# Attention maxima and sums handed over without DRAM, bulk transfers in pieces of 256 KB, and w1's stored parts in longer runs

## The chip, the cores and the metric

The kernel runs on one core of a Trainium2 chip. The core has five engines with a queue of instructions each: TensorE (PE; its weight loads are listed as PEld), VectorE (DVE), ScalarE (ACT), GpSimd (POOL) and SyncE (SP). Every DMA of this kernel is issued by SP. An engine works through its own queue in order, and waits for another engine or for a DMA by a semaphore. The metric is the time on the device of one execution, in microseconds (us), less is better.

## The reference

One transformer layer with an attention branch and an MLP branch that both start from the same normalized input and are added to the input. S = 2048 rows, D = 512 columns, H = 32 heads of 16, F = 1792 hidden units; all inputs and the output are float32.

```python
xn = _layernorm(x, axis=-1)
return x + _A_ref(xn, wqkv, wo) + _B_ref(xn, w1, b1, w2, b2)

# _A_ref
qkv = (xn @ wqkv).reshape(B, S, 3, H, Dh)                # q, k, v by head
scores = einsum("bhqd,bhkd->bhqk", q, k) * (Dh ** -0.5)
p = softmax(scores, axis=-1)
o = einsum("bhqk,bhkd->bhqd", p, v)
return o.reshape(B, S, D) @ wo

# _B_ref
h = gelu(xn @ w1 + b1)                                   # tanh form
return h @ w2 + b2
```

## The kernel before

**Numbers.** Products run in float16, with each float32 operand split into a high and a low part (suffix: index 0 and 1 of the dimension of 2), and three of the four part products are summed (`PAIRS`). The probabilities and v are multiplied in float32.

**Attention by tiles and units.** The 32 heads are taken in 8 groups of 4 (`NG`), the 2048 queries in 4 blocks of 512 (`NQB`): 32 *tiles* t = (g, qb). A tile has 16 *units*, 512 units in all (`NU`). Each unit does two things, for two different tiles. The first (`s_half`, four times) multiplies 128 queries with 512 keys and takes the row maxima with DVE (`mt`, L250). The second (`e_half`, four times) computes the scores again, transposed (128 keys by 512 queries, `pT`), and ACT takes the exponential (L295); `v_half` then multiplies by v into the bank `pV`. The second lags the first by `LEAD` = 20 units, so a tile's 16 units of maxima are done 4 units before its exponentials begin.

**How the maxima get there.** The maximum has to be subtracted from transposed scores, where it differs from column to column. It is done inside the product: the operand `qst` has for each head 64 rows, of which 62 and 63 hold the negative maximum in two float16 parts, and the same rows of `kst` hold the constant `MROW`. At a tile's last unit `s_end` reduces `mt` (128x64) to `mneg` (128x16). One slot later `store` (L264) transposes it on PE with two small products against `ident`, DVE writes the two parts `mhl` (L271, L272), two DMAs store them to DRAM (`m_d`, L275), and when these have landed four DMAs (L280) read rows 62 and 63 of the four heads back. The first `pT` product of the tile waits for them.

**How the sums get there.** v has a 17th column of ones, so row 16 of each head in `pV` is the sum of exponentials. `v_end` copies `pV` to `osb` (ACT, L321). Then, each in a slot of its own: `sums` (four DMAs to `den_d`, L333), a load of all sums as 64x32 into `dn` (L360), `inverse` (DVE, L336, and a store to `den_d`, L338), `spread` (four DMAs that copy each head's 512 reciprocals to 32 partitions of `rb`, L342), `store` (three steps on POOL, L346 to L348, result `ot`) and `put` (L353, to `ot_d`). `n` and `far` (L358) give the distances: 1, 2, 7, 10 and 13 slots after the tile's end, and 1, 2, 3, 5 and 7 in the last group of heads.

**Order.** From the 17th unit on the order on all five engines is written out by hand. `unit` (L582) emits one unit; `tick` (L226) follows each unit: it runs what `later(n, fn)` put down for this slot, then as many POOL steps of the list `pooled` as fit into `POOL_NS` = 2500 ns. A slot is a place in the program and no clock: SP issues an entry as soon as it has got there in its queue and what the entry reads or overwrites is free. `flush` (L231) ends a phase: it runs ticks with no unit between them until no local entry is left.

**What fills the PE beside attention.** `dense` puts up to four products per half unit of a `Group` into the half of the PE array that `v_half` leaves free. Three phases: the projections of q and k with `rest` (L853), beside which `prepare` (L880) loads, scales and splits w1, w2 and wo in 16 chunks of 512 KB (`chunk`, L641; three POOL steps each, L875 to L877) and stores the parts (`put`, L911: w1 to `w1_d`, w2 to `w2_d`); the MLP (`mlp`, L938), with its loads `fetch_x` (L532), `fetch_w1` (L537) and L971; and the product with wo (`tail`, L1072), whose operands `load_o` (L1005) reads for one block of 512 queries at a time in 8 DMAs, when `fetch_o` (L1065) finds that the block's last tile has been stored. `project` (L474) writes q and k by way of the buffers `stg`.

The first 16 units, with layer norm, transposition of x and the first projection, are ordered by the framework's own scheduler.

Of the kernel before, what the change touches and what calls it, by code (L numbers as in the profile page):

```python
# [8 lines left out]
F32 = mybir.dt.float32  # L9
# [38 lines left out]
def layer_kernel(ctx: ExitStack, tc: tile.TileContext, x, wqkv, wo, w1, b1, w2, b2, out):  # L48
# [16 lines left out]
    w1_d = dram.tile([NF, P, 2, NC, P], F16, name="w1_d")  # L65
    w2_d = dram.tile([P, 2, NF, D], F16, name="w2_d")
    acc_d = dram.tile([S, D], F32, name="acc_d")
    m_d = dram.tile([NG * NQB, 16, 2, P], F16, name="m_d")
    ot_d = dram.tile([D, 2, S], F16, name="ot_d")
    den_d = dram.tile([NG * NQB, 2, 4, QB], F32, name="den_d")  # L70
# [26 lines left out]
    mnegs = [const.tile([P, 32], F32, name=f"mneg{i}") for i in range(2)]  # L97
    for m in mnegs:
        nc.gpsimd.memset(m, 0.0)
# [153 lines left out]
    def s_end(u):  # L253
# [7 lines left out]
        nc.vector.tensor_reduce(mneg[:, :16], mt_of[t].rearrange("p h t k -> p (h t) k"), axis=AX.X, op=ALU.max, negate=True)  # L261
        given("dve", 220)

        def store():  # L264

            pt = banks("S")
            for a in range(2):
                nc.tensor.matmul(pt[32 * a:32 * a + 32, :64], mneg[64 * a:64 * a + 64, :],
                                 ident[64 * a:64 * a + 64, 64 * a:64 * a + 64], start=True, stop=True)
            mhl = work.tile([64, 2, 64], F16, name="mhl", bufs=2)  # L270
            nc.vector.tensor_scalar_mul(mhl[:, 0], pt[:64, :64], 1.0 / MROW)  # L271
            nc.vector.scalar_tensor_tensor(mhl[:, 1], pt[:64, :64], 1.0 / MROW, mhl[:, 0], op0=ALU.mult, op1=ALU.subtract)  # L272
            given("dve", 300)
            for a in range(2):
                nc.sync.dma_start(m_d[t, :, :, 64 * a:64 * a + 64], mhl[32 * a:32 * a + 16])  # L275
            for p in range(2):
                for a in range(2):
                    h = 2 * p + a
                    dst = qs[p][qb][64 * a + 62:64 * a + 64, :].rearrange("r (t q) -> r t q", q=P)
                    nc.sync.dma_start(dst, m_d[t, 4 * h:4 * h + 4].rearrange("t r q -> r t q"))  # L280
# [30 lines left out]
    def v_end(u):  # L311
# [19 lines left out]
        def sums():  # L331
            for h in range(4):
                nc.sync.dma_start(den_d[t, 0, h:h + 1, :], osb[32 * h + DH:32 * h + DH + 1, :])  # L333

        def inverse():
            nc.vector.reciprocal(dn, dn)  # L336
            given("dve", 330)
            later(1, lambda: nc.sync.dma_start(den_d[t, 1].rearrange("h (c q) -> (h c) q", q=32), dn))  # L338

        def spread():  # L340
            for h in range(4):
                nc.sync.dma_start(rb[32 * h:32 * h + 32, :], den_d[t, 1, h:h + 1, :].to_broadcast([32, QB]))  # L342

        def store():
# [4 lines left out]
                   (0, lambda: later(1 if n == 1 else 6, put)))  # L349
# [124 lines left out]
    def project(m, w, sb, wh, bank, early=False):  # L474
# [6 lines left out]
        def finish(pj):  # L481
# [4 lines left out]
            stg = ph.tile([P, 2, QB], F16, name="stg", bufs=2)  # L486
# [4 lines left out]
            else:  # L491
# [5 lines left out]
                else:  # L497
                    hi = lambda: nc.gpsimd.tensor_scalar(stg[:, 0], pf, 1.0, 0.0, op0=ALU.mult, op1=ALU.add)
                    lo = lambda: nc.gpsimd.tensor_tensor(stg[:, 1], pf, stg[:, 0], op=ALU.subtract)
                    later(1, lambda: pooled((620, hi), (1160, lo), (0, lambda: later(3, put, True))), True)  # L500
# [31 lines left out]
    def fetch_x(b):  # L532
        if b < NQB:
            xbs[b] = feed[0].tile([P, 2, NC, QB], F16, name="xb", bufs=1)
            nc.sync.dma_start(xbs[b], xn_d[:, :, :, b * QB:(b + 1) * QB])

    def fetch_w1(n):  # L537
        if n < NQB * NF:
            wcs[n] = feed[0].tile([P, 2, NC, P], F16, name="wc", bufs=3)
            nc.sync.dma_start(wcs[n], w1_d[n % NF])  # L540
# [89 lines left out]
    with ExitStack() as st1:  # L630
# [10 lines left out]
        def chunk(src):  # L641
            wf = ph.tile([P, 4 * W], F32, name="wch", bufs=3)
            v = wf.rearrange("p (a b) -> p a b", b=src.shape[2])
            nc.sync.dma_start(v, src)
# [235 lines left out]
        def prepare():  # L880
# [20 lines left out]
            for n in range(16):  # L901
# [9 lines left out]
                def put(wh, n):  # L911
                    if n < 7:
                        for a in range(2):
# [215 lines left out]
```

## Time and profile before

| what | us |
|---|---|
| three timed runs | 1566.6, 1568.99, 1570.97 (median 1568.99) |
| the profiled execution's own time | 1564.89 |
| its span, first to last instruction | 1563.1 |
| VectorE busy | 1424.6 (91%) |
| ScalarE busy | 1369.7 (88%) |
| GpSimd busy | 654.0 (42%) |
| bytes moved by DMA | 123.69 MB, mean 79 GB/s |

How to read the views. A *group* row names line, engine, operation, what it writes and reads, shapes and count; after the bar stand the busy time in us and the mean ns of one. A *windows* row gives, for a stretch of the span, its length and the busy us of PE, PEld, DVE, ACT and POOL with the number of instructions in brackets, then the mean clock that the throttle granted to TensorE (1.00 is full speed), the share of the 16 DMA engines that was busy, and GB/s. A *timeline* row gives the start in us, the duration in us, the engine, the line and the operation, how many like ones are merged, and in square brackets how long the engine stood idle before it and what ended that. SPq rows are DMA issues: their duration is the time that SP spent on the issue and not that of the transfer. A *waits* row gives who waited for whom: us in total, times, the longest. A row of *one line's view* gives the count and the shortest, median and longest duration in ns.

The slices of the page show that the DMA engines are busiest in the first fifth of the span (a share of 0.4 to 0.6), lightly used in the MLP (0.1 to 0.2), and somewhat more in the last eighth; PE stands at 90% or more in almost every slice.

### The profile page before, as it was taken

What the parts mean: (1) busy time and instruction counts of PE and PEld (TensorE: products, weight loads), DVE (VectorE), ACT (ScalarE), POOL (GpSimd) and SP (SyncE); (2) the same over time, 40 slices, a digit from 0 to 9 for tenths busy, and PEclk for the clock granted to TensorE, in tenths of its full rate; (3) what the DMA queues carried; (4) which work ended last, traced back from release to release, by engine and by line L of the source; (5) the groups of instructions that cost most, each with busy time, mean ns of one, the idle gap of its engine ahead of it and who ended that gap; (6) DMA issues with size and microseconds to landing.
All of it is one profiled execution on the core that took longest, in us unless ns stands there. A gap on an engine that the chain in (4) does not pass through costs nothing.

```text
span 1563.1 us, 85813 instructions
## 1 busy us (share of the span) xinstructions
PE 1513.9 (97%) x38915; PEld 810.6 (52%) x38915; DVE 1424.6 (91%) x2420; ACT 1369.7 (88%) x2254; POOL 654.0 (42%) x678
## 2 busy tenths in 40 slices
PE   8998989999999999999999999999999999999988
PEld 3434545555555555555555555555555555554433
DVE  8899878899999999999999999999999999998801
ACT  4317879999999999999999999999999999998983
POOL 3113667657771113768211277741137772110000
PEclk9999999999999999999999999999999999999999
DMA  6455665532221201131111211131012201002323
GB/s 205 129 154 187 206 159 189 168 96 78 69 62 60 61 27 42 42 81 42 49 28 47 63 42 32 48 89 36 28 49 61 56 22 35 26 21 87 105 72 111
DMA packets 120246, 123.69 MB, mean 79 GB/s; under 512 B 38988, under 2 KB 90572, under 8 KB 119880
## 3 DMA queue, kind: packets, MB, share of 16 engines
q1 hardware_dynamic: 119880, 118.21, 25.8%
q8 instruction: 304, 4.98, 1.4%
q14 instruction: 62, 0.51, 0.1%
HBM read 80.61 MB, written 37.34 MB: 75 GB/s over the span
## 4 chain that ended last, share of the span: by engine, by line
PE 73%; DVE 17%; DMA 4%; issue 3%; SPq 1%; POOL 1%; ACT 1%; DVEq 0%; POOLq 0%; ACTq 0%
PE pV L169 22%; PE pD L169 17%; PE pS L169 15%; PE pT L169 15%; DVE mt L250 12%; DVE hh L979 2%; DMA m_d<-mhl 1%; PE pD L426 1%; PE pT L426 1%; DMA oc<-ot_d 1%; PE pT L519 1%; SPq L392 1%; DVE amx L648 0%; POOL osb L346 0%; PE pV L519 0%
## 5 line engine op out<-in xcount | busy, mean ns | idle before, releaser
L295 ACT ACTIVATE pe<-pT,sexp 128x512 f32<-128x512 f32 x2048 | 1268.2, 687 | 80.8 <-PE pT L169 35.0
L250 DVE TENSOR_REDUCE mt<-pS 128x1 f32<-128x512 f32 x2048 | 1288.3, 683 | 38.4 <-PE pS L169 22.8
L169 PE MATMUL pV<-pe,vv 64*32 64x512 f32 x8192 | 1082.6, 598 | 2.0 <-issue 0.9
L169 PE MATMUL pT<-qst,kst 64*32 64x512 f16 x8192 | 709.9, 379 | 14.0 <-DMA qst<-m_d 8.9
L169 PE MATMUL pS<-kst,qst 62*32 62x512 f16 x8192 | 637.7, 379 | 19.9 <-DVE mt L250 15.9
L169 PEld LDWEIGHTS <-qst 62*32 62x32 f16 x8192 | 279.5, 92 | 253.1 <-issue 115.9
L169 PEld LDWEIGHTS <-kst 64*32 64x32 f16 x8192 | 294.6, 91 | 187.7 <-issue 76.3
L169 PE MATMUL pD<-w_s,g 64*32 64x512 f16 x5376 | 365.4, 377 | 0.4 <-issue 0.4
L169 PE MATMUL pD<-xb,wc 64*32 64x512 f16 x5376 | 360.8, 377 | 0.0
L169 PEld LDWEIGHTS pV<-pe,vv 64*32 64x32 f32 x8192 | 181.9, 105 | 101.6 <-PE pS L169 7.6
L169 PEld LDWEIGHTS <-wc 64*32 64x32 f16 x5376 | 120.1, 91 | 52.7 <-issue 1.9
L997 POOL TENSOR_TENSOR xa<-xa,yt 128x512 f32<-128x512 f32 x16 | 20.5, 1278 | 283.3 <-ACT yt L995 283.3
L169 PEld LDWEIGHTS <-g 64*32 64x32 f16 x5376 | 111.5, 91 | 46.1 <-issue 2.1
L346 POOL TENSOR_TENSOR osb<-osb,rb 128x512 f32<-128x512 f32 x31 | 39.9, 1286 | 223.6 <-DMA rb<-den_d 176.2
L169 PE MATMUL pD<-xt,wqk_h 64*32 64x512 f16 x1920 | 128.6, 380 | 0.6 <-issue 0.6
L959 POOL TENSOR_TENSOR t<-hh 128x512 f32<-128x512 f32 x56 | 58.3, 1041 | 144.4 <-DVE hh L979 130.3
L961 POOL TENSOR_TENSOR t<-t,hh 128x512 f32<-128x512 f32 x56 | 71.8, 1282 | 4.7
L954 POOL TENSOR_TENSOR t<-t,hh 128x512 f32<-128x512 f32 x56 | 71.7, 1280 | 4.7
L956 POOL TENSOR_TENSOR g<-t,g 128x512 f16<-128x512 f32 x56 | 65.3, 1165 | 4.7
L169 PEld LDWEIGHTS <-wqk_h 64*32 64x32 f16 x1920 | 44.1, 92 | 20.3 <-issue 5.1
L169 PE MATMUL pD<-wo_s,oc 64*32 64x512 f16 x768 | 53.0, 392 | 0.4 <-issue 0.2
L979 DVE TENSOR_SCALAR hh<-pD,fac,b_s 128x512 f32<-128x512 f32 x56 | 45.3, 809 | 1.2
(137 smaller groups left out, 817.7 us busy)
## 6 DMA issues: line engine op xcount, KB each, us to landing
wch<-in_B_w_dram SPq DMA_DIRECT2D x28, 512.0 KB
wc<-w_d SPq DMA_DIRECT2D x56, 256.0 KB
qk_d<-stg SPq DMA_DIRECT2D x32, 256.0 KB
rb<-den_d SPq DMA_DIRECT2D x124, 64.0 KB
kst<-qk_d SPq DMA_DIRECT2D x128, 48.0 KB
qst<-qk_d SPq DMA_DIRECT2D x128, 48.0 KB
xs<-in_A_x_dram SPq DMA_DIRECT2D x16, 256.0 KB
qk_d<-stg SPq DMA_DIRECT2D x32, 128.0 KB
```

Of the source, the lines that this page charges most:

```text
L169: p = nc.tensor.matmul(*args, **kw)
L250: nc.vector.reduce_max(mt_of[t][:, n, qt, kb:kb + 1], s, axis=AX.X)
L295: nc.scalar.activation(pe, st, AF.Exp, scale=sexp[:, g // 2:g // 2 + 1])
L346: pooled((1280, lambda: nc.gpsimd.tensor_tensor(osb, osb, rb, op=ALU.mult)), (620, lambda: nc.gpsimd.tensor_scalar(ot[:, 0], osb, 1.0, 0.0 ...
L392: nc.sync.dma_start((qst, kst)[w][g % 2][p][b][64 * a:64 * a + 48, :], qk_d[w, h * DH:(h + 1) * DH, :, b * QB:(b + 1) * QB].rearrange("d j ...
L426: nc.tensor.matmul(self.bank, lhs, rhs, start=start, stop=self.last and self.over())
L954: (1280, lambda: nc.gpsimd.tensor_tensor(t1, t1, hh, op=ALU.mult)),
L956: (1160, lambda: nc.gpsimd.tensor_tensor(g[:, 1, f, :], t1, g[:, 0, f, :], op=ALU.subtract)),
L959: pooled((1040, lambda: nc.gpsimd.tensor_tensor(t1, hh, hh, op=ALU.mult)), (620, lambda: nc.gpsimd.tensor_scalar(t1, t1, 1.0, 1.0 / GELU_A ...
L961: (1280, lambda: nc.gpsimd.tensor_tensor(t1, t1, hh, op=ALU.mult)),
L979: nc.vector.tensor_scalar(hh, hp, scale, bias, op0=ALU.mult, op1=ALU.add)
L997: add = lambda: nc.gpsimd.tensor_tensor(xa, xa, yt, op=ALU.add)
```

## The change

Its parts, by the places in the code before:

1. **Maxima.** `mneg` has the shape [128, 4, 2, 4]: the reduction reads `mt` twice by a broadcast and writes each maximum in two copies. The transposed result then has one row per head, part and block of 128 queries. A constant `parts` holds for each of these rows the factors that make it the high or the low part; it is filled by four memsets on POOL and one DMA from SBUF to SBUF at the start (the memsets of `mneg` go). DVE writes `mhl` [64, 64] with two instructions as before. Eight DMAs copy from `mhl` straight into rows 62 and 63 of `qst`, one for each head and each half of 128-query blocks. `m_d` is gone.
2. **Sums.** `sums` writes `dn` directly (SBUF to SBUF, four DMAs, one partition to 16 each); the load L360 is gone, the store of the reciprocals becomes an entry of its own (`keep`). The distances are 1, 5, 6, 8 and 11 slots, and 1, 3, 4, 5 and 7 in the last group.
3. **Pieces.** Chunks of weights are loaded in two halves, the second one slot later, once the unit number is 16 or more. xn is stored in 16 DMAs of 256 KB, three slots apart, and not in four of 1 MB. `fetch_x` reads four pieces of 256 KB in successive slots and not one of 1 MB. The last load of w2 is in four pieces, two slots apart. w2's parts are stored in two DMAs for each chunk. `load_o` spreads its eight DMAs over four slots for the first two blocks of queries; `fetch_o` starts a load only while the unit number modulo 16 is from 3 to 13, or after the last unit of maxima.
4. **w1's parts.** The buffer is laid out by column block, so that a part is stored in runs of 2 KB in two DMAs for each chunk, and not in runs of 256 B in four.
5. **Buffers.** `stg` has three buffers and not two, and its later store comes two slots after the POOL steps and not three.

```diff
@@ s_end
-        nc.vector.tensor_reduce(mneg[:, :16], mt_of[t].rearrange("p h t k -> p (h t) k"), axis=AX.X, op=ALU.max, negate=True)
+        nc.vector.tensor_reduce(mneg, mt_of[t].unsqueeze(2).to_broadcast([P, 4, 2, 4, 4]), axis=AX.X, op=ALU.max, negate=True)
...
-            mhl = work.tile([64, 2, 64], F16, name="mhl", bufs=2)
-            nc.vector.tensor_scalar_mul(mhl[:, 0], pt[:64, :64], 1.0 / MROW)
-            nc.vector.scalar_tensor_tensor(mhl[:, 1], pt[:64, :64], 1.0 / MROW, mhl[:, 0], op0=ALU.mult, op1=ALU.subtract)
+            mhl = work.tile([64, 64], F16, name="mhl", bufs=2)
+            nc.vector.tensor_scalar(mhl, pt[:64, :64], parts[:, 0:1], 0.0, op0=ALU.mult, op1=ALU.add)
+            nc.vector.scalar_tensor_tensor(mhl, pt[:64, :64], parts[:, 1:2], mhl, op0=ALU.mult, op1=ALU.add)
             given("dve", 300)
-            for a in range(2):
-                nc.sync.dma_start(m_d[t, :, :, 64 * a:64 * a + 64], mhl[32 * a:32 * a + 16])
-            for p in range(2):
-                for a in range(2):
-                    h = 2 * p + a
-                    dst = qs[p][qb][64 * a + 62:64 * a + 64, :].rearrange("r (t q) -> r t q", q=P)
-                    nc.sync.dma_start(dst, m_d[t, 4 * h:4 * h + 4].rearrange("t r q -> r t q"))
+            for h in range(4):
+                p, a = divmod(h, 2)
+                dst = qs[p][qb][64 * a + 62:64 * a + 64, :].rearrange("r (t x q) -> r t x q", x=2, q=64)
+                for x in range(2):
+                    nc.sync.dma_start(dst[:, :, x], mhl[32 * x + 8 * h:32 * x + 8 * h + 8])
@@ v_end
-                nc.sync.dma_start(den_d[t, 0, h:h + 1, :], osb[32 * h + DH:32 * h + DH + 1, :])
+                nc.sync.dma_start(dn[16 * h:16 * h + 16], osb[32 * h + DH:32 * h + DH + 1, :])
...
-        n, far = (2, 3) if t < (NG - 1) * NQB else (1, 0)
-        later(1, sums)
-        later(2, lambda: nc.sync.dma_start(dn, den_d[t, 0].rearrange("h (c q) -> (h c) q", q=32)))
-        later(2 + n + far, inverse)
-        later(3 + 2 * n + far, spread)
-        later(4 + 3 * n + far, store)
+        at = (1, 5, 6, 8, 11) if t < (NG - 1) * NQB else (1, 3, 4, 5, 7)
+        for k, fn in zip(at, (sums, inverse, keep, spread, store)):
+            later(k, fn)
@@ project
-            stg = ph.tile([P, 2, QB], F16, name="stg", bufs=2)
+            stg = ph.tile([P, 2, QB], F16, name="stg", bufs=3)
@@ fetch_x
-            nc.sync.dma_start(xbs[b], xn_d[:, :, :, b * QB:(b + 1) * QB])
+            for c in range(NC):
+                later(1 + c, lambda c=c: nc.sync.dma_start(xbs[b][:, :, c], xn_d[:, :, c, b * QB:(b + 1) * QB]))
@@ chunk
-            nc.sync.dma_start(v, src)
+            if pos[0] < 16:
+                nc.sync.dma_start(v, src)
+                return v
+            n = src.shape[1] // 2
+            nc.sync.dma_start(v[:, :n], src[:, :n])
+            later(1, lambda: nc.sync.dma_start(v[:, n:], src[:, n:]), True)
@@ rest
-            for c in range(NC):
-                later(9 + c, lambda c=c: nc.sync.dma_start(xn_d[:, :, c, :], xt[:, :, c, :]), True)
+            for k in range(4 * NQB):
+                c, cols = k % 4, slice(k // 4 * QB, k // 4 * QB + QB)
+                later(10 + 3 * k, lambda c=c, cols=cols: nc.sync.dma_start(xn_d[:, :, c, cols], xt[:, :, c, cols]), True)
@@ put, in prepare
-                    if n < 7:
-                        for a in range(2):
-                            for l in range(2):
-                                nc.sync.dma_start(w1_d[2 * n + a][:, l], wh[:, l, :, a * P:(a + 1) * P])
-                    elif n < 14:
-                        nc.sync.dma_start(w2_d[:, :, 2 * n - 14:2 * n - 12, :], wh)
+                    for a in range(2):
+                        if n < 7:
+                            later(a, lambda a=a: nc.sync.dma_start(w1_d[n, :, a], wh[:, a]), True)
+                        elif n < 14:
+                            later(a, lambda a=a: nc.sync.dma_start(w2_d[:, :, 2 * n - 14 + a], wh[:, :, a]), True)
@@ load_o
+        for k in range(8):
+            if qb < 2:
+                later(k // 2, lambda k=k: part(k))
+            else:
+                part(k)
@@ fetch_o
-                if (NG - 1) * NQB + (qb if qb < NQB - 1 else -1) in ready:
+                if (NG - 1) * NQB + (qb if qb < NQB - 1 else -1) in ready and (pos[0] >= NU or pos[0] % 16 in range(3, 14)):
```

More of the change, by code (lines that the diff above doesn't have):

```diff
@@ L970, in mlp @@
                 if b == 0 and f >= 3:
[L971 to L972 removed]
+                    for k in range(f - 3, NF if f == NF - 1 else f - 2):
+                        later(2 * (k - f + 3), lambda k=k: nc.sync.dma_start(w2_s[:, :, k], w2_d[:, :, k]))
                 if b == 0 and f == 3:
```

58 lines of the change are left out of this document (33 added, 25 removed).

## Prediction

> **What bounds the kernel now.** I read the page first, then stretches of the span (windows), then the waits, then the timeline around each long wait. The page's busy shares and its chain of waits:
>
> ```profile
> PE 1513.9 (97%) x38915; PEld 810.6 (52%) x38915; DVE 1424.6 (91%) x2420; ACT 1369.7 (88%) x2254; POOL 654.0 (42%) x678
> ...
> PE 73%; DVE 17%; DMA 4%; issue 3%; SPq 1%; POOL 1%; ACT 1%; DVEq 0%; POOLq 0%; ACTq 0%
> ```
>
> The reader is to see how little is left for a change to DMAs: 4% of the chain. A stretch in the middle shows three engines nearly full at once:
>
> ```profile
> 500.00:600.00 100.00, 99.82 (x2796) 57.23 (x2781) 98.62 (x163) 96.90 (x161) 12.50 (x11) 1.00 0.16 43
> ```
>
> There DVE has 1.4% to spare and no transfer is waited for, so nothing can be won, and DVE work that is added is paid. What can be won is where PE stands still for a DMA. The waits have it:
>
> ```profile
> PE pT L169 <- DMA qst<-m_d: 8.9, 3, 4.5
> ```
>
> Three times, two of them long, in 32 tiles. **The first** is at the tile that starts near 229 us (third of 32). DVE, SP and PE, each from its own timeline:
>
> ```profile
> 215.21 0.22 DVE L272 SCALAR_TENSOR_TENSOR mhl<-pS,mhl 64x64 f16<-64x64 f32 x1
> ```
> ```profile
> 216.59 0.37 SPq L644 DMA_DIRECT2D wch<-in_B_w_dram  x1
> ...
> 218.09 2.01 SPq L342 DMA_DIRECT2D rb<-den_d  x4
> 220.14 3.53 SPq L915 DMA_DIRECT2D w_d<-wsp  x4
> 223.77 1.22 SPq L275 DMA_DIRECT2D m_d<-mhl  x2
> 227.29 1.18 SPq L280 DMA_DIRECT2D qst<-m_d  x4
> ```
> ```profile
> 229.03 0.58 PE L169 MATMUL pT<-qst,kst 64*32 64x512 f16 x8 [4.50 <-DMA qst<-m_d]
> ```
>
> The maxima were ready at 215.4, but SP got to them at 223.8: it was held at the weight chunk until 216.6 and then had other issues ahead. PE wanted them at 229.03 - 4.50 = 224.5. **The second** is the last tile:
>
> ```profile
> 1481.18 0.22 DVE L272 SCALAR_TENSOR_TENSOR mhl<-pS,mhl 64x64 f16<-64x64 f32 x1
> ```
> ```profile
> 1474.15 3.17 SPq L1009 DMA_DIRECT2D oc<-ot_d  x4
> 1477.36 2.02 SPq L1014 DMA_DIRECT2D ac<-acc_d  x4
> 1479.48 2.84 SPq L1009 DMA_DIRECT2D oc<-ot_d  x4
> ...
> 1485.41 1.61 SPq L275 DMA_DIRECT2D m_d<-mhl  x2
> 1491.32 1.18 SPq L280 DMA_DIRECT2D qst<-m_d  x4
> ```
> ```profile
> 1493.07 0.63 PE L169 MATMUL pT<-qst,kst 64*32 64x512 f16 x8 [4.16 <-DMA qst<-m_d]
> ```
>
> Sixteen loads of two blocks stand ahead of the maxima, and the store then takes until 1491.3 to land behind them. PE wanted the maxima at 1488.9. **A third loss** is at the end of the MLP phase, where `flush` puts `sums` and `inverse` into the program with no unit between them, so DVE stands and PE behind it:
>
> ```profile
> 1404.40 1.12 SPq L333 DMA_DIRECT2D den_d<-osb  x4
> ```
> ```profile
> 1408.46 0.34 DVE L336 RECIPROCAL dn<-dn 64x32 f32<-64x32 f32 x1 [3.93 <-DMA dn<-den_d]
> ```
> ```profile
> 1409.41 0.40 PE L169 MATMUL pS<-kst,qst 62*32 62x512 f16 x4 [3.27 <-DVE mt L250]
> ```
>
> **What these three are worth.** A stall costs more than the idle time, since the granted clock falls after it. Windows over each (PE, PEld, DVE, ACT, POOL, clock), and one without a stall:
>
> ```profile
> 224.00:234.00 10.00, 5.50 (x113) 2.89 (x113) 2.98 (x5) 2.83 (x5) 8.60 (x9) 0.83 0.49 137
> ...
> 1404.00:1414.00 10.00, 6.73 (x112) 2.56 (x107) 5.30 (x10) 5.66 (x10) 0.09 (x1) 0.83 0.21 57
> ...
> 1488.00:1500.00 12.00, 7.80 (x140) 2.83 (x132) 0.75 (x1) 5.39 (x9) 0.00 (x0) 0.72 0.19 66
> 1500.00:1512.00 12.00, 11.93 (x308) 5.72 (x293) 1.80 (x3) 11.68 (x21) 0.00 (x0) 1.00 0.08 26
> ```
>
> First: 4.50 idle + 0.17 x 10 of clock = 6.2 us. Third: 3.27 + 1.7 = 5.0. Second: ACT sets the pace there; 11.68 - 5.39 = 6.3. Together 17.5 us, 1.1% of the time: the most that shorter waits can give.
>
> The Trainium skill ("TensorE: Matmul & The Clock Gate", Part 1) has the clock go back to half after an idle window of about 3.4 us. The trace nearly agrees: 3.27 us of idle was enough here. By that rule a third stall of 2.4 us, as it is worked out below, would leave the clock full, and the sum would be 1.7 us lower.
>
> **Part by part.** *Maxima.* What is removed: two stores, the wait for their landing, four reads. What is added: eight DMAs from SBUF to SBUF. The trace has no such DMA from `mhl`. Below it is bounded by the reads of the same rows from DRAM, 1.18 / 4 = 0.29 us of SP each; above by DMAs from SBUF into the same two rows:
>
> ```profile
> L88 SPq DMA_DIRECT2D kst<-ones_row x32: 615/622/861, 7.8 to 52.1; - x32
> ```
> ```profile
> 42.03 3.99 SPq L88 DMA_DIRECT2D kst<-ones_row  x6
> ```
>
> That is (3.99 - 0.62) / 5 = 0.67 us from one to the next. I take 0.67, since source, destination and size are nearest. In both stalls PE began 0.57 us after SP's last issue (229.03 - 228.47, 1493.07 - 1492.50). So a quiet tile's chain becomes 7 x 0.67 + 0.62 + 0.57 = 5.9 us. What it has:
>
> ```profile
> 530.68 0.22 DVE L272 SCALAR_TENSOR_TENSOR mhl<-pS,mhl 64x64 f16<-64x64 f32 x1
> ```
> ```profile
> 530.92 1.20 SPq L275 DMA_DIRECT2D m_d<-mhl  x2
> 533.35 1.15 SPq L280 DMA_DIRECT2D qst<-m_d  x4
> ```
> ```profile
> 537.86 0.39 PE L169 MATMUL pT<-qst,kst 64*32 64x512 f16 x4
> ```
>
> From 530.90 to 537.86: 7.0 us. Before, the chain ended at 534.50 + 0.57 = 535.1, with 2.8 us over; now 1.0 us is left. So in quiet tiles the new way is slower, and covered. Queued behind the eight issues on SP are bulk transfers and `spread`, wanted units later.
>
> *First stall.* SP is let go at 216.59; up to 218.09 it has the chunk and a store of q and k. w1's four issues become two (3.53 / 2 = 1.8 at this pace), the four of `rb` move two slots ahead. Then 219.9 + 5.3 + 0.6 = 225.8: a stall of 1.3, or 3.3 if `rb` is still in front. But SP was late because POOL was, and POOL waited for w1's stores:
>
> ```profile
> POOL wsp L876 <- DMA w_d<-wsp: 17.7, 7, 5.4
> ```
>
> With two stores in place of four these waits shrink, so the chunk comes earlier; in return a store starts one slot later. I leave 0.7 us of stall, without the clock: gain 5.5 (from 2.5 to 6.2).
>
> *Second stall.* `load_o` for the second block now puts four of its eight DMAs behind the maxima, so that twelve stand ahead and SP is there at 1482.4. Eight issues at 0.67, or at 1.61 / 2 = 0.81 as the stores had here, end at 1487.8 to 1488.9, and land by 1489.4, if a quarter less bulk is in front (16 loads took 1474.15 to about 1491: 1.1 us each, so twelve are through at 1487). I leave 0.5 us: gain 5.8. If the transfers queue as before, 4 us of stall remain: 0 to 6.3.
>
> *Third loss.* `dn` now needs one DMA step: 1404.40 + 3 x 0.67 + 0.62 + 0.57 = 1407.6 in place of 1408.46: gain 0.9. At L333's own pace (1.12 for four) it would be 1406.1, and with the clock kept 2.4 + 1.7 = 4.1. I take 0.9. Elsewhere `inverse` comes four slots after `sums`, some 10 us, and nothing waits.
>
> *Added on DVE.* The reduction to `mneg` reads 128 elements, not 64:
>
> ```profile
> L261 DVE TENSOR_REDUCE mneg<-mt 128x16 f32<-128x64 f32 x32 | 7.0, 219 | 1.1
> ...
> L648 DVE TENSOR_REDUCE amx<-wch 128x1 f32<-128x512 f32 x32 | 21.1, 674 | 0.4 <-DMA wch<-in_B_w_dram 0.4
> ```
>
> (674 - 219) / (512 - 64) = 1.02 ns an element: 65 ns x 32 = 2.1 us, of which I count 1.8 (DVE is full in most tiles; from 0, up to 7 if the time doubles). The two writes of `mhl` keep their shapes.
>
> *At the start.* One more DMA on SP among the first loads of x, which the first DVE work waits for: 0 to 0.67, I take 0.5.
>
> *Pieces, runs, buffers.* Some 60 more issues of 0.4 to 0.6 us, hidden in SP's idle time, but for what stands ahead of the maxima, counted above; the bytes stay. A third `stg` and fewer short packets help POOL, which bounds nothing (42%). Cost 0; uncovered, one issue ahead of a tile's maxima costs what exceeds the 1.0 us left. With the third short wait (8.9 - 4.50 - 4.16 = 0.2):
>
> Sum: 5.5 + 5.8 + 0.9 + 0.2 - 1.8 - 0.5 = 10.1 us. The profiled execution's own time is 1564.89, 4.1 below the median of the runs shown. It becomes 1554.8; from the median, **1558.9 us**.
>
> **The rivals.** *A: slower, by the eight issues.* Place: SP between `mhl` and the first `pT` of each tile. The chain is 8 issues + 0.57, and 7.0 less 0.07 of added DVE time is there, so it decides from (6.9 - 0.57) / 8 = 0.79 us an issue. At 0.90, a little above the longest L88 (0.861), the chain is 7.8, 0.9 us too long in some 28 tiles: 25 us, against 10 won: 1584. For it: issues near bulk are longer (0.81 at 1485). Against: the median is 0.62.
>
> The Trainium skill ("DMA: Bandwidth & Descriptors", Rules for kernel authors) speaks for this rival: small transfers should be coalesced, under 64 KB one pays mostly overhead. Its fit of 2.0 us for each DMA, if they ran one after the other, would by my estimate make the chain 16 us; the trace has four reads issued in 1.15 us, so they overlap.
>
> *B: it does not do what it says.* A slot is no clock: SP issues pieces back to back as it gets to them, and the same bytes stand ahead of the maxima at both stalls. Then 0.9 + 0.2 - 2.3 is left: 1570.2. For it: 16 loads left SP in 11 us without any pause. Against: at the last stall four loads are behind the maxima in the program itself.
>
> *C: more.* POOL catches up, all three losses and their clock go: 17.5 + 0.2 - 2.3 = 15.4: 1553.6, or 1549.5 from the profiled execution's own level.
>
> **How the numbers follow.** Forecast 0.60, A 0.12, B 0.13, C 0.15. A measurement here can tell 0.3%, or 4.7 us, from no change: faster is below 1564.3, slower above 1573.7. The forecast's own range is 1552 to 1565 (second stall gone or half kept, third with or without clock). For 8 in 10 C's lower end and B are taken in: 1549.5 to 1570.5; A is left out. Faster: nearly all of the forecast and C, 0.75; same: B and the forecast's edge, 0.14; slower: A, 0.11.
>
> **What would show it.** Right: no wait of `pT` for `qst` over 1.5 us, at the third and the last tile in particular; granted clock near 1.00 in 224 to 234 and in the twelve us after the last tile's start; SP's eight issues in about 5.3 us; the reduction to `mneg` near 285 ns; DVE's wait for `dn` near 3.1 us. Wrong: waits for `qst` of some tenths in many tiles (A); the same two long waits (B); a new wait of PE for w1, xn or `oc` pieces, or of DVE for `dn` outside `flush`, which I price at nothing.

## The result, and the profile after

| kernel | median, us | lowest to highest | runs |
|---|---|---|---|
| before | 1569.98 | 1566.6 to 1571.81 | 6 |
| after | 1587.2 | 1585.59 to 1591.72 | 6 |

The ratio after to before is 1.0119, with a 95% interval from 1.0099 to 1.014: the kernel is 1.2% slower, 17 us, where 10 us less was forecast. The profiled execution took 1591.51 us, its span is 1589.7 us, and its mean granted clock 0.985 (before 1564.89, 1563.1 and 0.995). The two profiled executions lie 26.6 us apart and the medians 17, so the traces account for a larger gap than the timed runs.

The chain of waits on the page of the kernel after:

```profile
PE 70%; DVE 17%; DMA 4%; issue 3%; SPq 3%; POOL 2%; ACT 1%; DVEq 0%; POOLq 0%; ACTq 0%
```

SP's queue has grown from 1% to 3% of the chain, POOL from 1% to 2%: a queue and an engine that bounded next to nothing before.

**Where in the span the time goes.** The reduction to `mneg` ends each tile's sixteen units, so its first and last start in a stretch date the tiles. The view of one tile name gives count, shortest, median and longest duration in ns, then the first and the last start in us. Before, for the first three tiles, the next two, and from the fifth tile to the end of the MLP phase:

```profile
L261 DVE TENSOR_REDUCE mneg<-mt x3: 202/220/220, 107.5 to 212.2; 128x16 f32<-128x64 f32 x3
...
L261 DVE TENSOR_REDUCE mneg<-mt x2: 219/220/221, 265.7 to 311.7; 128x16 f32<-128x64 f32 x2
...
L261 DVE TENSOR_REDUCE mneg<-mt x25: 210/220/221, 311.7 to 1346.5; 128x16 f32<-128x64 f32 x25
```

After:

```profile
L265 DVE TENSOR_REDUCE mneg<-mt x3: 274/286/286, 109.9 to 226.3; 128x32 f32<-128x128 f32 x3
...
L265 DVE TENSOR_REDUCE mneg<-mt x2: 286/286/287, 278.1 to 334.4; 128x32 f32<-128x128 f32 x2
...
L265 DVE TENSOR_REDUCE mneg<-mt x25: 275/286/289, 334.4 to 1371.3; 128x32 f32<-128x128 f32 x25
```

The kernel after is 2.4 us late at the first tile's end, 14.1 at the third's (226.3 - 212.2), 12.4 at the fourth's and 22.7 at the fifth's. Over the 24 tiles that follow it loses 2.1 us more (24.8 - 22.7). So nearly all of it is lost before 335 us, in the phase in which w1, w2 and wo are loaded, measured, split and stored, and in two places: in the second tile (its end is at 178.07, before at 164.04, so the 14 us are there by then), and around the start of the fourth tile's exponentials.

**The new waits.** Who waits for whom in the kernel after (us in total, times, the longest):

```profile
POOL wsp L885 <- DMA w_d<-wsp: 38.2, 9, 7.6
...
PE pT L173 <- DMA qst<-mhl: 8.8, 2, 6.7
...
DVE amx L656 <- DMA wch<-in_A_wo_dram: 4.5, 1, 4.5
DVE amx L656 <- DMA wch<-in_B_w_dram: 4.1, 2, 2.3
PE pD L173 <- DMA oc<-ot_d: 3.7, 1, 3.7
```

PE's total for the maxima is as it was, 8.8 for 8.9, but the waits are distributed otherwise: 2.08 at the third tile (4.50 before), 6.72 at the fourth and none at the last. POOL's for the split weights' buffer has doubled (17.7 before). The two lines on DVE and the last one on PE are new.

*The fourth tile.* SP, from its own timeline (start, duration):

```profile
278.73 0.33 SPq L651 DMA_DIRECT2D wch<-in_B_w_dram  x1
279.11 1.97 SPq L925 DMA_DIRECT2D w_d<-wsp  x1
281.18 1.95 SPq L347 DMA_DIRECT2D rb<-den_d  x4
283.17 0.52 SPq L925 DMA_DIRECT2D w_d<-wsp  x1
...
290.05 0.33 SPq L651 DMA_DIRECT2D wch<-in_A_wo_dram  x1
...
291.70 5.40 SPq L283 DMA_DIRECT2D qst<-mhl  x8
```

POOL, DVE and PE in the same stretch:

```profile
286.76 1.05 POOL L885 TENSOR_SCALAR wsp<-wch 128x1024 f16<-128x1024 f32 x1 [5.12 <-DMA w_d<-wsp]
287.89 2.13 POOL L886 TENSOR_TENSOR wsp<-wch,wsp 128x1024 f16<-128x1024 f32 x1
```
```profile
281.04 0.28 DVE L277 SCALAR_TENSOR_TENSOR mhl<-pS,parts,mhl 64x64 f16<-64x64 f32 x1
```
```profile
295.62 0.75 PE L173 MATMUL pT<-qst,kst 64*32 64x512 f16 x8 [6.72 <-DMA qst<-mhl]
```

Read them as a loop. The maxima lie in `mhl` at 281.3. In SP's queue a chunk's load (290.05) stands ahead of them; it needs the buffer that POOL is done with at 290.02 (287.89 + 2.13). POOL got there late because its step L885 waited 5.12 us for the stores of `wsp`, which SP issued at 279.11 and 283.17, behind the chunk load of 278.73, and the second of them behind `rb` as well. So the next turn of the loop waits for a store that was put behind the load of this turn: one turn takes from 278.73 to 290.05, 11.3 us, and the maxima sit in the queue for 10.4 of them (291.70 - 281.3). The granted clock (the third number from the end) falls behind the wait, as it did at the stalls of before:

```profile
290.00:302.00 12.00, 6.38 (x140) 3.84 (x148) 3.41 (x6) 4.48 (x8) 4.95 (x6) 0.72 0.47 144
```

*The second tile.* A chunk now comes in two halves, a slot apart, and DVE's `amx` needs both. SP, then DVE and PE:

```profile
121.33 5.23 SPq L283 DMA_DIRECT2D qst<-mhl  x8
126.60 3.65 SPq L394 DMA_DIRECT2D kst<-qk_d  x8
130.30 0.42 SPq L652 DMA_DIRECT2D wch<-in_B_w_dram  x1
```
```profile
133.19 0.69 DVE L656 TENSOR_REDUCE amx<-wch 128x1 f32<-128x512 f32 x1 [2.32 <-DMA wch<-in_B_w_dram]
...
152.64 0.69 DVE L656 TENSOR_REDUCE amx<-wch 128x1 f32<-128x512 f32 x1 [4.46 <-DMA wch<-in_A_wo_dram]
```
```profile
153.98 0.61 PE L173 MATMUL pS<-kst,qst 62*32 62x512 f16 x4 [4.72 <-DVE mt L254]
```

The half at 130.30 stands behind the first tile's eight maxima and eight loads of keys, 8.9 us of issuing. DVE works in order and cannot pass over `amx`, so the row maxima behind it come late, and PE waits 4.72 us for DVE to free a bank.

*The last tile.* SP and PE:

```profile
1501.92 2.56 SPq L1026 DMA_DIRECT2D oc<-ot_d  x4
1504.53 2.69 SPq L1029 DMA_DIRECT2D ac<-acc_d  x4
1507.33 2.50 SPq L1026 DMA_DIRECT2D oc<-ot_d  x4
1509.92 5.35 SPq L283 DMA_DIRECT2D qst<-mhl  x8
```
```profile
1512.15 1.04 PE L173 MATMUL pD<-wo_s,oc 64*32 64x512 f16 x8 [3.71 <-DMA oc<-ot_d]
```

PE no longer waits for the maxima, but for `oc`, which is loaded behind the eight DMAs of another block. Only the name of the wait has changed.

*What went as the prediction had it.* The eight issues in a quiet tile, the reduction, and the stretch from 500 to 600:

```profile
553.89 5.34 SPq L283 DMA_DIRECT2D qst<-mhl  x8
```
```profile
L265 DVE TENSOR_REDUCE mneg<-mt 128x32 f32<-128x128 f32 x32 | 9.1, 285 | 1.0
```
```profile
500.00:600.00 100.00, 99.69 (x2779) 56.12 (x2772) 98.49 (x165) 96.45 (x160) 16.75 (x15) 1.00 0.20 56
```

### The profile page after: what moved, and what is told of

It is laid out like the page before. It is cut to its first block, busy times and chain, and to the rows that moved or that the text cites. A ratio compares the mean times of both kernels' runs of the same rounds, so it can differ in the third digit from the quotient of the medians.

```text
span 1589.7 us, 86028 instructions
## 1 busy us (share of the span) xinstructions
PE 1526.6 (96%) x38915; PEld 816.2 (51%) x38915; DVE 1429.7 (90%) x2420; ACT 1372.2 (86%) x2254; POOL 654.1 (41%) x680
## 3 DMA queue, kind: packets, MB, share of 16 engines
q8 instruction: 304, 4.98, 1.3%
## 4 chain that ended last, share of the span: by engine, by line
PE 70%; DVE 17%; DMA 4%; issue 3%; SPq 3%; POOL 2%; ACT 1%; DVEq 0%; POOLq 0%; ACTq 0%
PE pV L173 21%; PE pD L173 16%; PE pS L173 15%; PE pT L173 14%; DVE mt L254 12%; DVE hh L992 2%; PE pD L428 1%; PE pT L428 1%; DMA w_d<-wsp 1%; DVE amx L656 1%; POOL wsp L886 1%; DMA rb<-den_d 1%; PE pT L521 1%; DMA oc<-ot_d 1%; PE pS L428 0%
## 5 line engine op out<-in xcount | busy, mean ns | idle before, releaser
L173 PE MATMUL pD<-xt,wqk_h 64*32 64x512 f16 x1920 | 133.3, 394 | 1.4 <-issue 1.4
```

The costliest lines, as they stand in the source:

```text
L173: p = nc.tensor.matmul(*args, **kw)
```

## The experiments

Two theories stood against each other. *H and L:* the time is lost in the pieces that wait for a slot: the chunks' second halves (H) and the stores of `w_d` (L). *A:* it is lost by the eight copies of the maxima, which keep SP 5.3 us in every tile. A third candidate was the third buffer `stg` (S). The kernel before is run beside each group: its median was 1568.06 (18 runs) beside the first four, 1567.51 (18) beside the next four and 1566.87 (19) beside the last four. The kernel after was not run again with these groups; its 1587.2 stands beside a median of 1569.98 for the kernel before. Differences from 1587.2 below may therefore be some 2 us too large; what each run is from the kernel before of its own group does not have this flaw.

**Chunks whole.** The kernel after, with

```diff
-            if pos[0] < 16:
-                nc.sync.dma_start(v, src)
-                return v
-            n = src.shape[1] // 2
-            nc.sync.dma_start(v[:, :n], src[:, :n])
-            later(1, lambda: nc.sync.dma_start(v[:, n:], src[:, n:]), True)
+            nc.sync.dma_start(v, src)
```

> The kernel after, with the weight chunks loaded whole again (one DMA of 512 KB in place of two halves, the second a slot later). Theory H (halves): in the changed kernel the second halves stand in SP's queue behind the eight issues of the first tile's maxima and behind q and k loads, and DVE's reductions over the weights wait for them (2.3 and 4.5 us at 133 and 153 us, with PE behind DVE). Whole again, these two waits go, units 20 to 26 are some 7 us earlier, and the time falls from 1587 to 1580 (1578 to 1582). The stall at the fourth tile (6.7 us) stays. Rival A (the eight issues themselves cost the time): nothing changes, 1586 to 1588.

Measured: 1578.05 us (5 runs), ratio to before 1.0077 (1.0051 to 1.0103); 9.1 below the kernel after (7.2, taken from each group's before). Neither of DVE's two waits shown above is there. The fourth tile's wait stays, at 7.0 us. The second tile's end is at 170.34 in place of 178.07. H holds, for the second tile.

**Stores at once.** The kernel after, with

```diff
-    later(a, lambda a=a: nc.sync.dma_start(w1_d[n, :, a], wh[:, a]), True)
+    nc.sync.dma_start(w1_d[n, :, a], wh[:, a])
...
-    later(a, lambda a=a: nc.sync.dma_start(w2_d[:, :, 2 * n - 14 + a], wh[:, :, a]), True)
+    nc.sync.dma_start(w2_d[:, :, 2 * n - 14 + a], wh[:, :, a])
```

> The kernel after, with the stores of w1's and w2's parts issued where they were before, two of them at once, and not one slot later. Theory L (loop): one slot later puts each store behind the load of the next chunk in SP's queue. That load waits for GpSimd to finish with a buffer, and GpSimd waits for the store to free another: a loop through the landing of a store, some 10 us a chunk where it was 8. So SP comes to the fourth tile's maxima 10 us late. Undone, GpSimd's waits for these stores fall from 38 us to under 18, the stalls at the third and fourth tile (2.1 and 6.7 us and the clock after them) go or stay under 1 us, and the time falls by 9 to 14 us, to 1573 to 1578. Rival A (eight issues) and a rival X (the sixteen stores of xn that stand between): the wait stays over 30 us and the time at 1585 to 1588.

Measured: 1571.29 us (10 runs), ratio 1.0025 (1.001 to 1.0041); 15.9 below the kernel after (14.0, taken from each group's before). Its waits:

```profile
POOL wsp L885 <- DMA w_d<-wsp: 17.0, 5, 4.7
...
PE pT L173 <- DMA qst<-mhl: 3.5, 2, 2.5
```

POOL's wait is back at what it was before, and of PE's waits for the maxima the one at the third tile is left, 2.5 us and 1.0 right behind it; the one at the fourth tile is gone. DVE's two waits for halves are still there. L holds, for the fourth tile.

**Two buffers `stg`.** The kernel after with `bufs=2` and `later(3, put, True)`, as before.

> The kernel after, with two buffers stg and their stores three slots after the GpSimd steps, as before. The first 16 units are 3 us later in the changed kernel, and nothing of the change but these buffers and the start-up constant lies there. Theory S: the third buffer changed the order that the framework's scheduler gives the first 16 units; with two, the 12th unit of maxima is at 89 us again and not at 92, and the time falls by 2 to 4 us, to 1583 to 1585. Rival: the constant's DMA or chance makes the 3 us, or two buffers bring back GpSimd's wait for stg of 18 us and lose as much: 1586 to 1590.

Measured: 1589.72 us (4 runs), ratio 1.0152 (1.0115 to 1.0189). The third buffer is no cause; POOL's wait for `stg` came back (29.0 us in total) and nothing depended on it. S falls.

**Maxima alone.** The kernel before with the direct copies of the maxima and `parts`, nothing else of the change.

> The kernel before, with the maxima alone handed over without DRAM (eight DMAs from SBUF to SBUF, the constant, the reduction that writes each maximum twice). Rival A (the eight issues take the time, a little in each tile): 1580 to 1588, with waits for the maxima of some tenths in many tiles. Theories H and L (the loss is in the pieces): 1568 to 1575: quiet tiles keep about 1 us to spare, the stall at the third tile grows to about 6 us, since SP is there at 224 as before and eight issues and a landing take 6.6 us, that at the last tile stays at 3 to 4, and the longer reduction costs 2.

Measured: 1576.62 us (8 runs), ratio 1.0059 (1.0036 to 1.0082): 8.6 slower than before, between the two ranges expected. But it is not in the way of A. The tiles' dates, in the same three stretches as above:

```profile
L265 DVE TENSOR_REDUCE mneg<-mt x3: 274/286/286, 110.6 to 224.6; 128x32 f32<-128x128 f32 x3
...
L265 DVE TENSOR_REDUCE mneg<-mt x25: 277/286/288, 319.6 to 1358.9; 128x32 f32<-128x128 f32 x25
```

The lead of the kernel before is 3.1 us at the first tile's end, 12.4 at the third's and 7.9 at the fifth's. In the 24 tiles after that it grows to 12.4 (1358.9 - 1346.5), 0.19 us a tile: more than the 0.07 forecast for DVE, and far from the 0.9 that A needs. The loss is in the second tile, whose end is at 176.61 (before 164.04). There PE twice waits for nothing that the profile shows, while the DMA engines are full or nearly so (the share is the second number from the end):

```profile
164.65 0.43 PE L173 MATMUL pT<-qst,kst 64*32 64x512 f16 x8 [1.96 <-issue]
172.50 0.61 PE L173 MATMUL pT<-qst,kst 64*32 64x512 f16 x4 [3.29 <-issue]
```
```profile
160.00:170.00 10.00, 7.24 (x204) 4.01 (x197) 8.10 (x19) 7.34 (x12) 4.05 (x5) 1.00 1.01 366
```

The two waits are 5.3 us of the 9.5 lost in this tile; behind the second the clock is 0.50 between 172 and 176. What PE waited for, and why these waits are longer than in the kernel before, no run shows.

**Both undone.** Whole chunks and stores at once together.

> Both halves of the loss undone together: the weights' chunks loaded whole again and the stores of w1's and w2's parts issued at once, all else as in the kernel after. Alone the first took 9.1 us off 1587.2 and the second 15.9. If the two are separate (one sits in the units up to the fifth tile on DVE, the other in the fourth tile's stall and POOL's cycle), they add: 1587.2 - 9.1 - 15.9 = 1562, and 1559 to 1566. If they are one cause seen twice (SP's queue behind the maxima), the second buys little: 1569 to 1572. By the trace: no wait of DVE for a chunk over 1 us after the sixteenth unit, no wait of PE for the fourth tile's maxima over 1 us, POOL's waits for wsp 17 us and not 38.

Measured: 1562.78 us (10 runs), ratio 0.997 (0.9956 to 0.9984). The two add up (1587.2 - 9.1 - 15.9 = 1562.2). With these two edits taken out, the rest of the change makes the kernel 4.7 us faster than before (1567.51 - 1562.78).

**Output loads at once.** The run before, and in `load_o` every piece issued at once, in the order of the blocks:

```diff
-            if qb < 2:
-                later(k // 2, lambda k=k: part(k))
-            else:
-                part(k)
+            part(k)
```

> As the run with whole chunks and stores at once, and the loads of the output's blocks (oc, ac) of the first two blocks issued at once instead of over four slots, so that they stand in SP's queue ahead of the third block's. If the 3.7 us wait of PE for oc at the end comes from that order, it goes, and with the clock that fell behind it 3 to 5 us: 1557 to 1559 where the run before it has 1562. If the wait only moves to the maxima of the last tile (PE waits for qst instead), the time falls by under 1 us.

Measured: 1560.96 us (9 runs), ratio 0.9956 (0.9944 to 0.9968); 1.8 less, between the two expectations and within the spread. The wait for `oc` is gone and part of it has become the old one:

```profile
1487.38 0.74 PE L173 MATMUL pT<-qst,kst 64*32 64x512 f16 x8 [2.57 <-DMA qst<-mhl]
```

Sixteen loads ahead of the maxima again, and the maxima wait, as before; twelve, and the loads do.

**`parts` late.** The run before, with the row and the copy that make `parts` moved from the constants to the line behind `clear(1)`, in the middle of the first 16 units.

> As the run with the output's loads at once, and the two columns of factors (parts) with the row behind them written and copied only in the second block of the preamble instead of ahead of the first loads. If the DMA that SP does at 7 us is what moves the first 16 units (a shift of 5 us by the seventeenth unit, a wait of DVE for a chunk of 2 us near 90 us, a granted clock of 0.9 behind it), that shift goes: 3 to 6 us off. If the order of the preamble alone, whatever moves it, sets the shift, or the buffers do, no change within 1 us.

Measured: 1557.23 us (4 runs), ratio 0.9933 (0.9909 to 0.9958); 3.7 less, which the spread does not settle: the four runs go from 1553.46 to 1561.25, and the profiled one is the slowest of them, 2.4 us above the profiled one of the run before. At the first tile's end the traces say more. It is at 108.2 us here, where the run before has 110.0 and the kernel before the change 107.5. Over all the kernels of this study it is at 109.9 to 111.4 in the seven that copy `parts` at the start, at 107.3 to 108.2 in six that copy it late or not at all, and at 110.1 in one that copies it late (the sums as before, below). So a DMA of 0.59 us on SP, at 6.98 us and ahead of a load of the first weights, mostly goes with some 2 us at the first tile's end. The granted clock of 0.89 between 100 and 116 us (before: 1.00) is still there, so the DMA isn't what causes that; what does was not found.

**Four copies.** The run before, and the maxima by one product over 128 rows and four copies of 8 rows by 128:

```diff
-            for a in range(2):
-                r = slice(64 * a, 64 * a + 64)
-                nc.tensor.matmul(pt[32 * a:32 * a + 32, :64], mneg[r].rearrange("p h i t -> p (h i t)"),
-                                 ident[r, r], start=True, stop=True)
-            mhl = work.tile([64, 64], F16, name="mhl", bufs=2)
+            nc.tensor.matmul(pt[:32, :P], mneg.rearrange("p h i t -> p (h i t)"), ident, start=True, stop=True)
+            mhl = work.tile([32, P], F16, name="mhl", bufs=2)
...
-                for x in range(2):
-                    nc.sync.dma_start(dst[:, :, x], mhl[32 * x + 8 * h:32 * x + 8 * h + 8])
+                nc.sync.dma_start(dst, mhl[8 * h:8 * h + 8])
```

> As the run with parts late, and the maxima go by one product over all 128 rows and four copies of 8 rows x 128 instead of two products and eight copies of 8 x 64. If an issue keeps its 0.67 us whatever the row, the chain from the reduction to the last landing is 2.7 us shorter, and the wait left at the third tile (2.5 us where the stores are at once) goes: 2 to 4 us off. If what is left there is SP arriving late, not the chain, under 1 us; if four copies with rows twice as long take twice as long each, none.

Measured: 1554.67 us (4 runs), ratio 0.992 (0.9892 to 0.9947): 0.8% faster than the kernel before and the fastest median but one of the study. The copies' view (count, shortest, median, longest in ns), and the one wait for the maxima that is left, at the last tile:

```profile
L275 SPq DMA_DIRECT2D qst<-mhl x128: 610/614/742, 118.9 to 1489.0; - x128
```
```profile
1489.71 0.41 PE L169 MATMUL pT<-qst,kst 64*32 64x512 f16 x8 [1.82 <-DMA qst<-mhl]
```

A row twice as long does not lengthen the issue. Of four waits of PE for the maxima in the run before (6.4 us together) one is left. The intervals of each of the last three steps overlap with those of the step ahead of it; for the three together, 8.1 us, they do not. What each gives alone the times do not settle; the traces show what each one changed.

**Stores late, alone.** The other way round: the kernel before, with its stores of w1 and w2 one slot later and nothing else.

```diff
                 def put(wh, n):
+                    later(0, lambda: now(wh, n), True)
+
+                def now(wh, n):
                     if n < 7:
```

> The kernel before with one thing of the change alone: the stores of w1's and w2's parts wait for the next slot, whole as they were. If the cycle of POOL's steps, chunk load, store and landing is what the slot lengthens, with the maxima still going through DRAM, POOL's longest wait for wsp grows past 7 us, the maxima of the fourth tile come late and the kernel is 8 to 16 us slower than 1568: 1576 to 1584. If the loss needs the eight copies of the maxima in SP's queue as well, within 3 us of 1568.

Measured: 1580.12 us (4 runs), ratio 1.0088 (1.0066 to 1.011): 13.3 slower, with the maxima still going through DRAM. POOL's waits, and PE at the fourth tile:

```profile
POOL wsp L876 <- DMA w_d<-wsp: 36.7, 9, 7.7
```
```profile
294.57 0.64 PE L169 MATMUL pT<-qst,kst 64*32 64x512 f16 x8 [6.98 <-DMA qst<-m_d]
```

These are the waits of the kernel after, 38.2 and 6.72. L needs nothing else of the change.

**Halves, alone.** The kernel before, with its chunks in halves as in the kernel after.

> The kernel before with the other thing alone: the weights' chunks loaded in two halves a slot apart from the seventeenth unit on. If the second half's place in SP's queue behind any waiting issue is enough, DVE's waits for it in the first two tiles (2.3 and 4.5 us in the kernel after) are there and the time is 5 to 9 us above 1568: 1573 to 1577. If it takes the eight copies of the maxima ahead of the half to make it late, within 3 us of 1568.

Measured: 1562.4 us (10 runs), ratio 0.9979 (0.9967 to 0.9991): 4.5 less than before, so no loss at all, and outside both expectations. The half that came late is issued at 124.52 here, in place of 130.30:

```profile
116.89 1.28 SPq L275 DMA_DIRECT2D m_d<-mhl  x2
119.35 1.19 SPq L280 DMA_DIRECT2D qst<-m_d  x4
120.59 3.89 SPq L392 DMA_DIRECT2D kst<-qk_d  x8
124.52 0.42 SPq L649 DMA_DIRECT2D wch<-in_B_w_dram  x1
```

So H takes a second edit beside the halves. The rows point to the maxima, which keep SP 5.2 us where they kept it 2.5 (1.28 + 1.19); no run had these two alone. Why the halves by themselves are faster was not followed up.

**Sums as before.** The kernel with four copies, its sums through DRAM again (`sums` to `spread` as in the kernel before).

> The kernel with four copies of the maxima (whole chunks, stores at once, output loads at once, parts late), but the sums of exponentials through DRAM as in the kernel before. If the sums' direct way brings nothing outside the flush and there nothing either, within 1.5 us of that kernel's 1554.7. If it brought the 0.9 us that I gave it in the flush, 0.5 to 1.5 us more; if it also keeps SP's queue shorter in every tile, 2 to 4 us more.

Measured: 1553.53 us (4 runs), ratio 0.9915 (0.989 to 0.994), the same within the spread. The sums' direct way is worth nothing that the times show. In the profiled executions DVE's wait for `dn` in `flush` is 4.03 us, and 3.53 with the direct sums.

**The rest whole.** The kernel with four copies, with x stored in 4 and loaded in whole blocks, and w2 in its old pieces.

> The kernel with four copies of the maxima, and the other bulk transfers whole as before: x's parts (xn) stored in 4 and loaded whole, w2 loaded in its old pieces. If the pieces cost nothing and bring nothing outside the weights' chunks and stores, within 1.5 us of 1554.7. If smaller pieces let short transfers through, 2 to 4 us slower; if each issue costs SP time that something waits for, 1 to 3 us faster.

Measured: 1560.9 us (10 runs), ratio 0.9963 (0.9951 to 0.9975): 6.2 slower by the medians, more than the 2 to 4 expected at most. The profiled executions differ by 2.1 us alone, and show one place: with x's stores whole the DMA engines are full between 160 and 170 us (a share of 1.00, as in the run with the maxima alone) and PE stands 2.63 us for "issue". With four copies and x in pieces the same window has a share of 0.43:

```profile
160.00:170.00 10.00, 8.20 (x232) 4.60 (x223) 8.17 (x16) 7.72 (x13) 5.81 (x6) 1.00 0.43 141
```

So storing x in pieces probably helps a little; the size, from 2 to 6 us, stays open, and the loads of x and w2 were not taken apart from the stores.

## Why the prediction was wrong

**The step that failed** is "Pieces, runs, buffers", and in it "Cost 0". Two edits of that paragraph cost 24.4 us (1587.2 - 1562.78; 21.9, taken from each group's before), against 10.1 of gains in the whole sum. I asked of every piece whether it stands ahead of a tile's maxima, and covered the rest by SP's idle time. What I left out is that SP waits in order, and that some of those transfers close a loop: POOL's step frees the chunk's buffer, SP loads the next, then stores the split parts, and POOL's next step waits for that store. The prediction even has the sentence "a store starts one slot later", under the first stall, and gave it no price. In that slot the next chunk's load slips ahead of the store in SP's queue, and it waits for POOL: 13.3 us for that alone, with nothing else changed. The other edit, the halves, fails the other way round: a half does not stand ahead of the maxima but behind them, and DVE waits for it (9.1 us in this kernel, and nothing in the kernel before). The paragraph's other sentence, "POOL, which bounds nothing (42%)", is the error in short: POOL bounds nothing by its work, but a step of it that waits holds SP, and SP holds the maxima.

**First stall.** Forecast: 0.7 us left, out of bounds of 1.3 and, with `rb` in front, 3.3, less what earlier chunks would bring. At the third tile PE waits 2.08 us, so the bounds held; but "the chunk comes earlier" is wrong: POOL's waits grew from 17.7 to 38.2, and a stall of 6.72 stands one tile on. With the stores at once it is gone.

**Second stall.** Twelve transfers stand ahead of the maxima and PE no longer waits for these, as forecast. That the four moved behind them carry the products that PE wants next was named among what would show me wrong, "a new wait of PE for w1, xn or `oc` pieces", and priced at nothing. Of the 5.8 us nothing came (PE waits 3.71 us for `oc`, where it waited 4.16 for the maxima); undoing the order brings 1.8, within the spread.

**Third loss.** Forecast 0.9. SP and DVE in `flush`:

```profile
1429.43 2.73 SPq L336 DMA_DIRECT2D dn<-osb  x4
```
```profile
1433.42 0.34 DVE L339 RECIPROCAL dn<-dn 64x32 f32<-64x32 f32 x1 [3.86 <-DMA dn<-osb]
```

The issues take 2.73 us, by my step 2.63. But from the last issue's end to DVE it is 1.26 us (1433.42 - 1432.16) and not the 0.57 that I carried over from the maxima. The wait is 3.86 for 3.93, PE stands 3.20 for 3.27, and taking the direct sums out changes no time. With four copies the wait is 3.53, and 4.03 without the direct sums: 0.5 at best, of the 0.9. Where the prediction says that with the clock kept the sum would be 1.7 lower, that is right for the time only: the sum of the gains would be 1.7 higher.

**Added on DVE.** 9.1 - 7.0 = 2.1 us in all, 285 ns each, as forecast (1.8 counted).

**At the start.** 0.5 was probably too small: the first tile ends 2.4 us late, and moving that DMA brings 3.7 by the medians of few runs.

**Rival A** gave 1584, nearer to the measured time than the forecast, and is wrong all the same. It decided from 0.79 us an issue; the kernel after has 0.61 at the median and 0.73 at the longest, the quiet tile's eight issues take 5.34 us, and 24 tiles lose 2.1 us together, little more than the 1.6 that the longer reduction costs there (24 x 0.065). The eight issues do harm where something that is wanted soon stands behind them in the queue, as the chunks' halves in the second tile. That the copies alone cost 8.6 us, in the second tile and not in each, neither the forecast nor A had, and its cause stays open. The Trainium skill ("DMA: Bandwidth & Descriptors", Rules for kernel authors) advises to coalesce small transfers; the run with four copies in place of eight agrees in direction, 2.6 us by the medians, within the spread. The 2.0 us for each DMA that the prediction takes from the same page of the Trainium skill (Anatomy of one DMA) is fitted there to DMAs that GpSimd issues. Here SP issues every one, and the quiet tile's eight are issued in 5.34 us, far below the 16 worked out from that figure.

Without the two edits the change is worth 4.7 us, half of the sum; with the order of the output loads and of `parts` put right, 10.3 (1567.51 - 1557.23). That this is close to the forecast 10.1 is chance: it is not made up of the forecast's terms.

## What to carry to other kernels

When a transfer is moved by one slot, write down who waits for its landing and what then waits for that engine's next step: if the path comes back to the same queue, the slot is paid once a turn. An in-order queue that issues everything turns each wait of a "free" engine into a wait of whatever stands behind it, so busy shares say nothing about the cost of moving an issue. A piece that must land with its other half gains nothing by being issued apart from it when a long run of small issues can get in between; without such a run the halves did no harm here.

## What the runs showed of the hardware

**The clock can fall after less than I had assumed.** The third tile's wait in the kernel after, and the four us behind it:

```profile
241.58 0.75 PE L173 MATMUL pT<-qst,kst 64*32 64x512 f16 x8 [2.08 <-DMA qst<-mhl]
```
```profile
242.00:246.00 4.00, 4.00 (x87) 2.30 (x76) 1.98 (x3) 2.40 (x4) 3.83 (x4) 0.64 0.47 140
```

The four us behind the last tile's 1.82 us with four copies, whose row stands above:

```profile
1492.00:1496.00 4.00, 3.96 (x112) 2.10 (x100) 0.00 (x0) 4.00 (x9) 0.00 (x0) 1.00 0.00 0
```

The wait of 2.08 us, with another of 0.96 some six us ahead of it, was followed by a clock of 0.64, and the one of 2.57 us with the output loads at once by 0.68 (1488 to 1492); the one of 1.82 left it at 1.00. But in the run with the stores at once a wait of 2.53 us, up to 237.19, left it at 1.00 all through 232 to 252. The Trainium skill ("TensorE: Matmul & The Clock Gate", Part 1) speaks of an idle window of about 3.4 us; by these rows about 2 us can be enough, and 2.5 need not be. So the length of one wait does not decide, and whether a stall of 2.4 us would have left the clock full, as the prediction has it by that rule, stays open.

**An issue's price differs with what is copied.** Eight rows out of `mhl` in SBUF cost SP 0.61 us or more, at 64 or at 128 elements a row; the four reads of the same maxima out of DRAM took 1.19 us together, 0.30 each. But where it copies from does not decide: the same rows of `osb` in SBUF took 1.12 us for four on the way to DRAM, 0.28 each, and 2.73 for four when each was spread over 16 partitions of `dn`. Rows, partitions and the side of the copy were not taken apart.

**PE's longer "issue" waits came with full DMA engines, but full engines are not enough.** In the runs with the maxima alone and with the rest whole, both with x's stores whole, PE stood 1.96, 3.29 and 2.63 us for nothing that the profile shows, at or just after a DMA share of 1.00. In the kernel before, the share is 0.98 to 1.03 from 152 to 168 us too, and PE stands 0.88 us for "issue" there at the longest. The page lists a queue of the kind "instruction" with 4.98 MB beside the data queues. That PE was waiting for its instructions there is a guess; no run tried it.
